# Stage A of a Fourier filter on quarters of the TensorE array: four matmuls per unit, eight units per batch

## The chip, the cores and the metric

The kernel runs on one core of one Trainium2 chip. A core has a matrix engine (TensorE, PE in the profile, with its weight loads as PEld), three engines for elementwise work (VectorE or DVE, ScalarE or ACT, GpSimd or POOL) and a queue processor, SyncE or SP, that issues DMAs here. The metric is the time of one execution on the device in microseconds; less is better. Every time below comes from runs of the kernel on the chip or from one profiled execution of it.

## The reference

A filter in the frequency domain along the sequence, and then a feed-forward network with a squared ReLU on all 24,064 tokens:

```python
batch, seq, dim = (8, 3008, 256)
X = np.fft.rfft(x, axis=1)
F = (filt_r + 1j * filt_i)[None, :, :]
y = np.fft.irfft(X * F, n=x.shape[1], axis=1).astype(np.float32)
...
h = np.maximum(y.reshape(24064, 256) @ w_in, 0.0)     # w_in 256 x 2048
out = (h * h @ w_out).astype(np.float32)              # w_out 2048 x 256
```

## The kernel before

The transform of length 3008 is split as 64 x 47. It runs per batch in stages, each of small matmuls by constant matrices, with a trip through memory where the data have to be laid out anew:

- **Stage A** is the transform of length 47. A row n of the sequence is cut as n = 64 n2 + 32 h + m, with n2 from 0 to 46, h of 0 or 1 and m from 0 to 31. A tile of x holds the 94 pairs (n2, h) in its partitions, and eight values of m with 256 channels each in its free dimension. The constant matrix `sSA` (94 x 96) has the same 47 x 48 block twice, one for each h, and zeros elsewhere. One unit is one matmul of 512 columns (two values of m) into one PSUM bank, and one copy to fp16. Four units fill a tile `u` of eight values of m (a chunk), which `write_u` stores to `dU` in memory. A batch has 16 units in four chunks.
- **Stage B** (`unit_b`, 12 units per batch) is the transform of length 64 on what `read_u` reads back: two matmuls of 256 columns into one bank, which VectorE multiplies with the filter; two accumulating DMAs from POOL's queue then add the halves.
- **Stage P** (`unit_p`, 12 units) is the first half of the inverse: two matmuls of 256 columns into one bank, a copy by ScalarE, a store to `dZ`.
- **Stage Y** (`unit_y`, 16 units) is the last transform: four matmuls of 94 columns into one bank, and a copy by ScalarE or VectorE into the operand `yt` of the network.

The network runs over 47 groups of 512 tokens, each in 8 slots. A slot s has the first product for one group (`ffn_g1`: four or more matmuls with 512 columns in all to each of two banks psH, then a ReLU by ScalarE, line 557), and a part of the second product for the group before it (`products`, 112 matmuls of 128 columns in the eight slots of a group; the sums that it needs, `sums`, and the squares, `ffn_sq`, are VectorE's).

The order of all engines' work is written out by hand, in the loop at the end: in each slot first `ffn_g1`, then a first place for units of the transform, then `products`, then a second place, then sums and squares. A place is half a slot. `fft_plan` fills the places: every unit has a due time in slots, at most one unit goes to a half-slot, the nearest free one, with a penalty for crowded neighbourhoods; units of stages B, P and Y are placed ahead of those of stage A. `moves` (loads of x, reads of `dU` and `dZ`) go to their half-slot without this limit. Batches 0 and 1 take stage A from wider tiles in the part before the loop; of batch 1 only four units of stage A are in the plan.

All units of the transform take their PSUM bank from one pool, `psF`, which has two banks and gives them in turn. The other six banks belong to `ffn_g1` (psH, twice two) and to the second product (psO, two). A unit's matmuls wait until the bank they are given has been read out by the unit that had it before.

x is loaded by POOL's DMA queue, which turns it to fp16 on the way: `load_x`, two DMAs for each chunk, each with 96 partitions and four values of m (a contiguous piece of 4 KB per partition); the last batch has 94 rows and cuts each in two. Stage A's copies are ScalarE's from batch 3 on, and by turns ScalarE's and VectorE's in batch 2. The stores of u go to the SP queue, one DMA of 96 partitions for each chunk.

Lines that matter below: 195 to 199 (loads of x), 208 (`sSA`), 340 to 343 (store of u), 358 (stage A's matmul), 362 and 364 (its copies), 442 and 450 (stage B's matmul and multiply), 487 and 489 (stage P), 523, 530 and 532 (stage Y), 553 and 557 (first product and ReLU), 564 (square), 639 to 648 (sums), 666 (second product), 710 to 719 (due times).

Of the kernel before, what the change touches and what calls it, by code (L numbers as in the profile page):

```python
# [9 lines left out]
F16 = mybir.dt.float16  # L10
# [8 lines left out]
N1, N2, NC, NM = 64, 47, 24, 32  # L19
# [7 lines left out]
def _build_consts():  # L27
    N = N1 * N2
    n2 = np.arange(N2)
    m = np.arange(NM)  # L30


    SA = np.zeros((N2, 2, 2, 2, NC))
    for c in range(NC):
        for h in range(2):
            SA[:, h, h, 0, c] = np.cos(2 * np.pi * n2 * c / N2)
            SA[:, h, h, 1, c] = np.sin(2 * np.pi * n2 * c / N2)

    S0 = np.zeros((128, 6, 2, 48))
    for h in range(2):
        q = SA[:, h, h].reshape(N2, 48)
        for t in range(2):
            S0[2 * h + t::4, t, h] = q[:32]
        for c in range(4):
            S0[4 * h + c:120:8, 2 + c, h] = q[32:]


    freq = np.full((NC, 64), -1)  # L50
    for c in range(NC):
        for j in range(32):
            freq[c, j] = 47 * j + c
            if c:
                freq[c, 32 + j] = 47 * j + 47 - c
    freq[0, 32] = N // 2


    SB = np.zeros((NM, 2, 2, NC, 2, 64))

    n1j = 8 * (m % 8) + 2 * (m // 8)
    SP = np.zeros((2, 64, NC, 2, 2, NM))
    for c in range(NC):
        for f in range(64):
            k = freq[c, f]
            if k < 0:
                continue
            sg = 1.0 if (f < 32 or c == 0) else -1.0
            for h in range(2):
                th = 2 * np.pi * ((k * (32 * h + m)) % N) / N  # L70
                SB[:, h, 0, c, 0, f] = np.cos(th)
                SB[:, h, 1, c, 0, f] = -sg * np.sin(th)
                SB[:, h, 0, c, 1, f] = -np.sin(th)
                SB[:, h, 1, c, 1, f] = -sg * np.cos(th)
            if c == 0 and f == 32:
                SB[:, :, 1, c, :, f] = 0.0
            w = (1.0 if k in (0, N // 2) else 2.0) / N
            for i in range(2):
                th = 2 * np.pi * ((k * (n1j + i)) % N) / N
                cs, sn = w * np.cos(th), w * np.sin(th)  # L80
                SP[0, f, c, i, 0] = cs
                SP[0, f, c, i, 1] = sg * sn
                SP[1, f, c, i, 0] = -sn
                SP[1, f, c, i, 1] = sg * cs


    SY = np.zeros((32, 2, 2, N2, 2))
    for c in range(NC):
        th = 2 * np.pi * c * n2 / N2
        for i in range(2):  # L90
            SY[c + c // 12 * 4, i, 0, :, i] = np.cos(th)
            SY[c + c // 12 * 4, i, 1, :, i] = -np.sin(th)


    PF = np.zeros((128, 6, 2, 2, 32))
    for w, (s, q) in enumerate(PQ):
        for j in range(32):
            PF[4 * j + q, w, :, s, j] = 1.0

    f16 = lambda a, p: np.ascontiguousarray(a.reshape(p, -1).astype(np.float16))  # L100
    C0 = np.zeros((128, 1472))
    C0[:, 0:576] = S0.reshape(128, 6, 2, 2, NC).transpose(0, 1, 4, 2, 3).reshape(128, 576)
    C0[:, 576:704] = np.eye(128)
    C0[:, 704:1280] = S0.reshape(128, 576)
    C0[0:94, 1280:1376] = SA.reshape(94, 96)
    C0[:, 1376:1470] = SY.reshape(128, 94)
    return f16(C0, 128), f16(PF, 128), f16(SB, 128), f16(SP, 128)

# [2 lines left out]
def kernel(  # L111
# [9 lines left out]
    nc = tc.nc  # L121
    B, S, D = x.shape
# [18 lines left out]
    p_x16 = ctx.enter_context(tc.tile_pool(name="p_x16", bufs=4))  # L141
    p_u = ctx.enter_context(tc.tile_pool(name="p_u", bufs=3))
# [10 lines left out]
    xrows = x.rearrange("b s d -> (b s) d")  # L153
    dU = [dram.tile([NM * 96, D], F16, name=f"dU{b}") for b in range(B)]
    dZ = [dram.tile([NM * 96, D], F16, name=f"dZ{b}") for b in range(B)]

    def psF(name):
        return pps.tile([128, 512], F32, tag="psF", name=name, bufs=2)
# [25 lines left out]
    x16s, us, uts, prods, zes, zts, yts = {}, {}, {}, {}, {}, {}, {}  # L184

    def load_x(b, k):

        c, i = divmod(k, 2)
        if i == 0:
            x16s[(b, c)] = p_x16.tile([96, 8, D], F16, tag="x16", name=f"x16_{b}_{c}")  # L190
        t = x16s[(b, c)][:, 4 * i:4 * i + 4, :]
        m = slice(8 * c + 4 * i, 8 * c + 4 * i + 4)
        if b + 1 < B:
            v = xrows[b * S:b * S + 96 * NM, :].rearrange("(p m) d -> p m d", m=NM)
            nc.gpsimd.dma_start(out=t, in_=v[:, m, :])
        else:
            v = xrows[b * S:b * S + S, :].rearrange("(p m) d -> p m d", m=NM)
            nc.gpsimd.dma_start(out=t[0:80], in_=v[0:80, m, :])
            nc.gpsimd.dma_start(out=t[80:94], in_=v[80:94, m, :])

    sC0 = p_t.tile([128, 1280], F16, tag="t", name="sC0")
    sC1 = const.tile([128, 192], F16, name="sC1")
    nc.scalar.dma_start(out=sC0[:, 0:704], in_=dC0.ap()[:, 0:704])
    s0 = sC0[:, 0:576].rearrange("p (w q) -> p w q", q=96)
    s1 = sC0[:, 704:1280].rearrange("p (w q) -> p w q", q=96)
    sSA = sC1[0:94, 0:96]
    sSY = sC1[0:112, 96:190]
    ident = sC0[:, 576:704]  # L210
    sPF = p_out.tile([128, 6, 128], F16, tag="ost", name="sPF")
# [1 line left out]
    xw32, xw16 = {}, {}  # L213
# [56 lines left out]
    ps = psO("warm").rearrange("p a d -> p (a d)")  # L270
# [67 lines left out]


    def write_u(b, c):  # L340
        nc.sync.dma_start(
            out=dU[b].rearrange("(m q) d -> q m d", q=96)[:, 8 * c:8 * c + 8, :],
            in_=us.pop((b, c)))

    def unit_a(b, a):

        c, i = divmod(a, 4)
        if i == 0:
            us[(b, c)] = p_u.tile([96, 8, D], F16, tag="u", name=f"u_{b}_{c}")
        ps = psF(f"psA_{b}_{a}")  # L350
        m = slice(2 * i, 2 * i + 2)
        if b == 1:
            nc.tensor.matmul(ps[0:96, :], s1[:, c // 2, :], xw16[(b, 2 * (c % 2))][:, m, :],
                             start=True, stop=False)
            nc.tensor.matmul(ps[0:96, :], s1[0:120, 2 + c, :], xw16[(b, 1)][0:120, m, :],
                             start=False, stop=True)
        else:
            nc.tensor.matmul(ps[0:96, :], sSA, x16s[(b, c)][0:94, m, :], start=True, stop=True)  # L358
        o = us[(b, c)][:, 2 * i:2 * i + 2, :]
        pv = ps[0:96, :].rearrange("p (a d) -> p a d", d=D)  # L360
        if a % 2 == 0 or b > 2:
            nc.scalar.copy(out=o, in_=pv)  # L362
        else:
            nc.vector.tensor_copy(out=o, in_=pv)
        if i == 3:
            write_u(b, c)

    def chunk_a(b, c):
# [323 lines left out]
    def fft_plan():  # L692

        fixed, units, moves = [], [], []
        for b in range(1, B):
            f = (b * S // TG) * SLOTS - (48 if b > 1 else 40)
            d = 0
            if b == 1:
                for n in range(4, 16):
                    fixed.append(((n if n < 8 else n + 2 if n < 12 else 2 * n - 7) + n % 2 / 2,  # L700
                                  unit_y, 0, n))
                moves.append((7.5, read_z, 0, 3))
                for k in range(4):
                    moves.append(((4.5, 5.5, 7.5, 7.5)[k], cast_wout, k, nc.vector))
                for a in range(12, 16):
                    fixed.append((2 + a / 2, unit_a, b, a))
                moves.append((10.5, read_u, b))
                d = 7
            else:
                for a in range(16):  # L710
                    if a % 2 == 0 and b > 2:
                        moves.append((f + ((-57 + 2.3 * a) if b == 3 else (-66 + 2.75 * a)),
                                      load_x, b, a // 2))
                    units.append((f + (-16 + a, -46 + 2.1 * a, -56 + 2.75 * a)[min(b, 4) - 2],
                                  unit_a, b, a))
                moves.append((f + (2 if b == 2 else -6.5), read_u, b))
            for p in range(12):
                r = 13.5 + 15 * p / 11 if b == 1 else 6 + 28 * p / 11 if b == 2 else -2 + 36 * p / 11
                units.append((f + r, unit_b, b, p))
                if b == 1 and 2 <= p < 10:  # L720
                    moves.append((f + r, load_x, 2, p - 2))
                units.append((f + r + (4.5 if b == 1 else 7 - 2.5 * p / 11), unit_p, b, p))
            for c in range(4):
                moves.append((f + (40 + d / 14, 43, 48, 54)[c] - d, read_z, b, c))
            for n in range(16):
                (fixed if n < 4 else units).append((f + YN[n] - d, unit_y, b, n))
        work, used, done = {}, set(), {}
        for r, *u in fixed:
            h = int(2 * r)
# [29 lines left out]
    for k in range(2):  # L759
        c = slice(12 * k, 12 * k + 12)  # L760
# [62 lines left out]
    for s in range((NG + 1) * SLOTS):  # L823
        g, k = divmod(s, SLOTS)
# [46 lines left out]
```

## Time and profile before

| what | value |
|---|---|
| median of 3 runs | 764.0 us (763.1 to 764.0) |
| the profiled execution, its own time | 765.4 us |
| its span, first to last instruction | 763.6 us |
| mean granted TensorE clock | 0.997 |
| stage A of batches 2 to 7 on TensorE (line 358) | 96 matmuls, 97 to 558 us into the span |
| its copies: ScalarE (line 362, with two of batch 1) / VectorE (line 364, with two of batch 1) | 90 of 580 ns / 10 of 681 ns |
| multiply of stage B (line 450) | 84 of 1219 ns |
| copy of stage P (line 489) | 84 of 584 ns |
| ReLU of the first product (line 557) | 376 of 1024 ns |
| load of x, issue to landing | median 5.0 us |
| DMA traffic | 109.26 MB, 143 GB/s in the mean |

A group of the profile is all instructions of one line, engine and shape: its count, its busy time, the mean time of one, and the time its engine was idle just before them with the instruction that ended the idle time. "PE psB L442" as a releaser means that the engine waited for the matmuls of line 442. The timeline lists instructions by their start, in microseconds from the start of the span. A matmul's duration is from its entry to its modelled end, and neighbours overlap: what it costs the stream is the distance to the next start.

### The profile page before, as it was taken

Reading aid. Unit: us, or ns where it says so; the run is one execution under the profiler, and the core shown is the slowest. Engines: PE = TensorE matmul, PEld = TensorE weight load, DVE = VectorE, ACT = ScalarE, POOL = GpSimd, SP = SyncE. Lnnn points to the kernel's source line nnn. Section 1 sums busy time; section 2 is a strip of 40 time slices with the busy share of each in tenths; the row PEclk is TensorE's granted clock in tenths of the full one; section 3 lists DMA queues with packets and bytes.
Section 4 is the critical chain, followed back from the end, with each engine's and each line's share of the span. In section 5 each row is a group of like instructions: output and inputs, shape, how many; then the busy total and the mean of one; then the engine's idle time right before and its main releaser. Section 6 shows DMA issues by size and latency. Waiting matters only on the chain.

```text
span 763.6 us, 19701 instructions
## 1 busy us (share of the span) xinstructions
PE 749.8 (98%) x8262; PEld 552.9 (72%) x8262; DVE 645.8 (85%) x714; ACT 578.8 (76%) x841; POOL 192.4 (25%) x260
## 2 busy tenths in 40 slices
PE   8988999999999999999999999999999999999998
PEld 5845766777777777877778777787777777777776
DVE  5857998899889888988979898798989989888783
ACT  3966777888877887788877877877877777777773
POOL 3800750244222321222312324033311222000000
PEclk9999999999999999999999999999999999999999
DMA  9985798765786467745585656775447334321011
GB/s 364 391 229 182 115 173 214 208 115 117 154 218 133 89 123 172 191 102 125 115 211 123 120 120 115 201 147 109 101 122 198 89 72 99 98 76 50 29 57 57
DMA packets 104946, 109.26 MB, mean 143 GB/s; under 512 B 9640, under 2 KB 93096, under 8 KB 102936
## 3 DMA queue, kind: packets, MB, share of 16 engines
q1 hardware_dynamic: 85704, 87.38, 37.1%
q0 software_dynamic: 19008, 20.43, 20.3%
q8 instruction: 65, 1.06, 0.6%
q14 instruction: 25, 0.20, 0.1%
q10 hardware_dynamic: 144, 0.18, 0.1%
HBM read 58.12 MB, written 48.23 MB: 139 GB/s over the span
## 4 chain that ended last, share of the span: by engine, by line
PE 88%; DVE 6%; DMA 3%; ACT 1%; issue 1%; POOL 0%; SPq 0%; ACTq 0%; DVEq 0%
PE psH L553 39%; PE psX L666 20%; PE psY L666 14%; PE psB L442 3%; PE psY L523 2%; PE psA L358 2%; PE psP L487 2%; DVE h L564 2%; PE psO L573 2%; DVE prod L450 1%; DMA ut<-dU 1%; PE warm L272 1%; DMA dU<-u 1%; PE psf L291 1%; PE psf L294 1%
## 5 line engine op out<-in xcount | busy, mean ns | idle before, releaser
L557 ACT ACTIVATE h<-psH 128x1024 f16<-128x1024 f32 x376 | 384.6, 1024 | 151.6 <-PE psH L553 147.4
L553 PE MATMUL psH<-yt,sWin 128*128 128x512 f16 (+7 forms) x1728 | 388.3, 352 | 1.4 <-DVE yt L532 0.6
L564 DVE TENSOR_TENSOR h<-h 128x2048 f16<-128x2048 f16 (+1 forms) x192 | 229.8, 1197 | 48.3 <-ACT h L557 48.0
L457 POOL DMA_DIRECT2D prod<-prod x168 | 138.6, 965 | 438.0 <-DVE prod L450 429.1
L553 PEld LDWEIGHTS <-sWin 128*128 128x128 f16 x1728 | 152.2, 98 | 99.4 <-issue 4.8
L666 PEld LDWEIGHTS <-sum 128*128 128x128 f16 x2880 | 177.5, 98 | 20.2 <-issue 0.2
L666 PEld LDWEIGHTS <-h 128*128 128x128 f16 x2160 | 133.6, 98 | 21.0
L450 DVE TENSOR_TENSOR prod<-psB,sF 128x1024 f16<-128x1024 f32 x84 | 102.4, 1219 | 16.4 <-PE psB L442 16.2
L666 PE MATMUL psX<-sT,sum 128*128 128x128 f16 x1440 | 102.5, 219 | 0.0
L666 PE MATMUL psY<-sT,sum 128*128 128x128 f16 x720 | 69.7, 219 | 0.0
L642 DVE TENSOR_TENSOR sum<-sum,h 128x2048 f16<-128x2048 f16 x45 | 55.0, 1222 | 1.0
L666 PE MATMUL psY<-sWout,h 128*128 128x128 f16 x720 | 55.0, 219 | 0.0
L666 PE MATMUL psX<-sT,h 128*128 128x128 f16 x720 | 54.9, 219 | 0.0
L666 PE MATMUL psY<-sWout,sum 128*128 128x128 f16 x720 | 54.7, 219 | 0.1
L645 DVE TENSOR_TENSOR sum<-h 128x2048 f16<-128x2048 f16 x45 | 54.8, 1217 | 0.0
L648 DVE TENSOR_TENSOR sum<-h,sum 128x2048 f16<-128x2048 f16 x45 | 54.7, 1217 | 0.0
L639 DVE TENSOR_TENSOR sum<-h 128x2048 f16<-128x2048 f16 x45 | 54.7, 1215 | 0.0
L362 ACT CAST u<-psA 96x512 f16<-96x512 f32 x90 | 52.2, 580 | 3.2 <-PE psA L358 2.8
L532 DVE CAST yt<-psY 128x376 f16<-128x376 f32 x62 | 33.7, 544 | 20.0 <-PE psY L523 19.9
L489 ACT CAST ze<-psP 128x512 f16<-128x512 f32 x84 | 48.9, 584 | 0.6 <-PE psP L487 0.4
L666 PE MATMUL psX<-sWout,h 128*128 128x128 f16 x720 | 47.6, 219 | 0.0
L523 PEld LDWEIGHTS <-zt 112*128 112x128 f16 x512 | 33.5, 98 | 18.5 <-issue 4.3
(86 smaller groups left out, 644.4 us busy)
## 6 DMA issues: line engine op xcount, KB each, us to landing
zt<-dZ SPq DMA_DIRECT2D x64, 192.0 KB
dU<-u SPq DMA_DIRECT2D x28, 384.0 KB
prod<-prod POOLq DMA_DIRECT2D x168, 64.0 KB, 2.7
dZ<-ze SPq DMA_DIRECT2D x28, 384.0 KB
x<-in_x_dram POOLq DMA_DIRECT2D x40, 192.0 KB, 5.0
ut<-dU SPq DMA_DIRECT2D x7, 1024.0 KB
xw<-in_x_dram SPq DMA_DIRECT2D x6, 1024.0 KB
out_dram<-top SPq DMA_DIRECT2D x31, 128.0 KB
```

The lines of the kernel that those rows point to most:

```text
L362: nc.scalar.copy(out=o, in_=pv)
L450: nc.vector.tensor_mul(out=prod, in0=ps.rearrange("p (a d) -> p a d", d=D).unsqueeze(1).to_broadcast([128, 2, 2, D]), in1=sF[:, :, 2 * p:2 ...
L457: nc.gpsimd.dma_start(out=prod[64 * i:64 * i + 64, 0], in_=prod[64 - 64 * i:128 - 64 * i, 1], accum_op=mybir.AluOpType.add)
L489: nc.scalar.copy(out=zes[(b, c)][:, 2 * i6:2 * i6 + 2, :], in_=ps.rearrange("p (a d) -> p a d", d=D))
L553: nc.tensor.matmul(ps[:, i, o:o + n], sWin[:, dt, jt * 128:(jt + 1) * 128], yts[b][:, dt, r:r + n], start=(dt == 0), stop=(dt == 1))
L557: nc.scalar.activation(out=h2[:, 2 * s:2 * s + 2, :], in_=ps, func=AF.Relu)
L564: nc.vector.tensor_mul(out=v, in0=v, in1=v)
L639: nc.vector.tensor_add(out=t, in0=a21, in1=a22)
L642: nc.vector.tensor_sub(out=t, in0=f[5], in1=a11)
L645: nc.vector.tensor_sub(out=t, in0=a11, in1=a21)
L648: nc.vector.tensor_sub(out=t, in0=a12, in1=f[6])
L666: nc.tensor.matmul(o[:, t, :], f[p][:, q, 128 * t:128 * t + 128], sg["w"][p][:, q, :], start=(m == 0 and p in (1, 2)), stop=(q == 7), skip ...
```

## The change

The array of TensorE is used in quarters in stage A of batches 2 to 7. The tile of x now has h = 0 in partitions 0 to 46 and h = 1 in partitions 64 to 110 (`load_x` issues one DMA for each h, of 48 partitions with eight values of m each; the last batch again in two pieces). The weight is the 47 x 48 block alone, once in each half of the partitions, with 16 columns of zeros to 64. A unit has four matmuls of 512 columns: for j of 0 and 1 (which four of the chunk's values of m) and h of 0 and 1. They read partitions from 64 h on and write PSUM partitions from 64 j on, h = 0 into a first bank of psF and h = 1 into a second one. Two copies follow, one for each bank, of 112 partitions by 512 elements. A chunk has two units, a batch eight in place of sixteen; in the plan they take the due times of the old units of odd number. `write_u` stores a chunk by two DMAs of 48 partitions. Batch 1 keeps the old unit under the name `unit_a1` and the old store, and its units of stages B and P, with the loads of x for batch 2 that go with them, come half a slot later (13.5 becomes 14).

```diff
@@ constants
-    C0[0:94, 1280:1376] = SA.reshape(94, 96)
+    for h in range(2):
+        C0[64 * h:64 * h + N2, 1280:1328] = SA[:, h, h].reshape(N2, 48)
...
-    sSA = sC1[0:94, 0:96]
+    sSA = sC1[:, 0:64]
@@ load_x
-        c, i = divmod(k, 2)
-        if i == 0:
-            x16s[(b, c)] = p_x16.tile([96, 8, D], F16, tag="x16", name=f"x16_{b}_{c}")
-        t = x16s[(b, c)][:, 4 * i:4 * i + 4, :]
-        m = slice(8 * c + 4 * i, 8 * c + 4 * i + 4)
-        if b + 1 < B:
-            v = xrows[b * S:b * S + 96 * NM, :].rearrange("(p m) d -> p m d", m=NM)
-            nc.gpsimd.dma_start(out=t, in_=v[:, m, :])
-        else:
-            v = xrows[b * S:b * S + S, :].rearrange("(p m) d -> p m d", m=NM)
-            nc.gpsimd.dma_start(out=t[0:80], in_=v[0:80, m, :])
-            nc.gpsimd.dma_start(out=t[80:94], in_=v[80:94, m, :])
+        c, h = divmod(k, 2)
+        if h == 0:
+            x16s[(b, c)] = p_x16.tile([112, 8, D], F16, tag="x16", name=f"x16_{b}_{c}")
+        t = x16s[(b, c)]
+        n = 48 if b + 1 < B else N2
+        v = xrows[b * S:b * S + 64 * n, :].rearrange("(n h m) d -> h n m d", h=2, m=NM)[h]
+        for p0, p1 in ((0, n),) if n == 48 else ((0, 32), (32, n)):
+            nc.gpsimd.dma_start(out=t[64 * h + p0:64 * h + p1],
+                                in_=v[p0:p1, 8 * c:8 * c + 8, :])
@@ write_u (b > 1)
+        v = dU[b].rearrange("(m q) d -> q m d", q=48)
+        for j in range(2):
+            m = 16 * c + 8 * j
+            nc.sync.dma_start(out=v[:, m:m + 8, :], in_=u[64 * j:64 * j + 48])
@@ unit_a
-            nc.tensor.matmul(ps[0:96, :], sSA, x16s[(b, c)][0:94, m, :], start=True, stop=True)
...
+    def unit_a(b, a):
+
+        c, i = divmod(a, 2)
+        if i == 0:
+            us[(b, c)] = p_u.tile([112, 8, D], F16, tag="u", name=f"u_{b}_{c}")
+        ps = [psF(f"psA_{b}_{a}_{h}") for h in range(2)]
+        for j in range(2):
+            m = slice(4 * j + 2 * i, 4 * j + 2 * i + 2)
+            for h in range(2):
+                p = slice(64 * h, 64 * h + N2)
+                nc.tensor.matmul(ps[h][64 * j:64 * j + 64, :], sSA[p], x16s[(b, c)][p, m, :],
+                                 start=True, stop=True)
+        for h in range(2):
+            o = us[(b, c)][:, 4 * i + h:4 * i + h + 3:2, :]
+            pv = ps[h][0:112, :].rearrange("p (a d) -> p a d", d=D)
+            if h == 0 or b > 2:
+                nc.scalar.copy(out=o, in_=pv)
+            else:
+                nc.vector.tensor_copy(out=o, in_=pv)
+        if i == 1:
+            write_u(b, c)
@@ fft_plan
-                    units.append((f + (-16 + a, -46 + 2.1 * a, -56 + 2.75 * a)[min(b, 4) - 2],
-                                  unit_a, b, a))
+                    if a % 2:
+                        units.append((f + (-16 + a, -46 + 2.1 * a, -56 + 2.75 * a)[min(b, 4) - 2],
+                                      unit_a, b, a // 2))
...
-                r = 13.5 + 15 * p / 11 if b == 1 else 6 + 28 * p / 11 if b == 2 else -2 + 36 * p / 11
+                r = 14 + 15 * p / 11 if b == 1 else 6 + 28 * p / 11 if b == 2 else -2 + 36 * p / 11
```

More of the change, by code (lines that the diff above doesn't have):

```diff
@@ L340, in write_u, with unit_a1 @@
     def write_u(b, c):
[L341 to L345, printed above, removed]
+        u = us.pop((b, c))
+        if b == 1:
+            nc.sync.dma_start(
+                out=dU[b].rearrange("(m q) d -> q m d", q=96)[:, 8 * c:8 * c + 8, :], in_=u)
+            return
+        v = dU[b].rearrange("(m q) d -> q m d", q=48)
+        for j in range(2):
+            m = 16 * c + 8 * j
+            nc.sync.dma_start(out=v[:, m:m + 8, :], in_=u[64 * j:64 * j + 48])
+    def unit_a1(b, a):
         c, i = divmod(a, 4)
@@ L351, in unit_a @@
         m = slice(2 * i, 2 * i + 2)
[L352 to L358, printed above, removed]
+        nc.tensor.matmul(ps[0:96, :], s1[:, c // 2, :], xw16[(b, 2 * (c % 2))][:, m, :],
+                         start=True, stop=False)
+        nc.tensor.matmul(ps[0:96, :], s1[0:120, 2 + c, :], xw16[(b, 1)][0:120, m, :],
+                         start=False, stop=True)
         o = us[(b, c)][:, 2 * i:2 * i + 2, :]
         pv = ps[0:96, :].rearrange("p (a d) -> p a d", d=D)
-        if a % 2 == 0 or b > 2:
+        if a % 2 == 0:
             nc.scalar.copy(out=o, in_=pv)
@@ L705, in fft_plan @@
                 for a in range(12, 16):
-                    fixed.append((2 + a / 2, unit_a, b, a))
+                    fixed.append((2 + a / 2, unit_a1, b, a))
                 moves.append((10.5, read_u, b))
```

## The prediction

> **What bounds the kernel now.** I read the page first: busy shares, then the chain that ended last.
>
> ```profile
> PE 749.8 (98%) x8262; PEld 552.9 (72%) x8262; DVE 645.8 (85%) x714; ACT 578.8 (76%) x841; POOL 192.4 (25%) x260
> ...
> PE 88%; DVE 6%; DMA 3%; ACT 1%; issue 1%; POOL 0%; SPq 0%; ACTq 0%; DVEq 0%
> ```
>
> TensorE is busy for 98% of the span and carries 88% of the chain. A busy share can hide slow matmuls, so I then asked for the chain in order of time, in the middle of the run:
>
> ```profile
> 381.63 0.86 PE psH L553 x4
> ...
> 384.25 0.89 PE psX L666 x16
> ```
>
> Four 512-column matmuls take 0.86 us (215 ns each), sixteen of 128 columns 0.89 us (56 ns each). I take these as the rate of a dense stream. The table of windows shows that the stream has no holes where the changed units run (97 to 558 us):
>
> ```profile
> 200.00:290.00 90.00, 89.85 (x1015) 66.53 (x1013) 78.59 (x86) 71.89 (x108) 23.41 (x32) 1.00 0.64 144
> 290.00:381.00 91.00, 90.85 (x1030) 68.17 (x1028) 79.87 (x88) 72.85 (x109) 24.05 (x32) 1.00 0.62 140
> ```
>
> The columns are stage, length, busy time of PE, PEld, DVE, ACT and POOL, clock and DMA. In 181 us TensorE lacks 0.3 us; DVE has 12% left, ACT 20%. So here a nanosecond taken from the matmul stream is a nanosecond of the total, and a nanosecond that TensorE waits is lost and nothing makes it good. The changed group is small in it (the groups by line: busy us, mean ns, idle time before and its releaser; with it the copy that empties its bank, and stage B's multiply):
>
> ```profile
> L450 DVE TENSOR_TENSOR prod<-psB,sF 128x1024 f16<-128x1024 f32 x84 | 102.4, 1219 | 16.4 <-PE psB L442 16.2
> ...
> L362 ACT CAST u<-psA 96x512 f16<-96x512 f32 x90 | 52.2, 580 | 3.2 <-PE psA L358 2.8
> ...
> L358 PE MATMUL psA<-x,sC 94*96 94x512 f16 x96 | 36.6, 381 | 0.2 <-DVE u L364 0.2
> ```
>
> The 381 ns is one matmul from entry to modelled end; the stream advances 215 ns. The 96 matmuls hold TensorE for 96 x 215 = 20.6 us, and each waits for almost nothing (0.2 us in all). Last, the timeline, because the new unit takes both psF banks at once and there are only two. This is a stage-B unit followed one half-slot later by a stage-A unit of an odd number, which is where the change puts a new unit:
>
> ```profile
> 243.70 1.22 DVE L645 TENSOR_TENSOR sum<-h 128x2048 f16<-128x2048 f16 x1
> 243.71 0.38 PE L442 MATMUL psB<-ut,sSB 128*128 128x256 f16 x2
> ...
> 244.71 0.38 PE L358 MATMUL psA<-x,sC 94*96 94x512 f16 x1
> ...
> 244.84 1.22 DVE L450 TENSOR_TENSOR prod<-psB,sF 128x1024 f16<-128x1024 f32 x1
> 244.93 1.03 PE L553 MATMUL psH<-yt,sWin 128*128 128x512 f16 x4
> ...
> 246.11 0.33 PE L523 MATMUL psY<-sC,zt 112*128 112x94 f16 x4 [0.15 <-DVE prod L450]
> ```
>
> The A matmul starts at 244.71, when the bank of the B unit is still full: VectorE reads it until 244.84 + 1.22 = 246.06. It doesn't matter today, since A has the other bank. The next unit (Y) needs B's bank, and it starts at 246.11, 0.05 us after VectorE is done and 0.15 us late. That is the price of a bank in this kernel, seen once.
>
> **What the Trainium skill says.** "TensorE: Matmul & The Clock Gate", Part 3: matmuls in different row and column tiles run at the same time, span about one matmul plus 4 ns for each further tile (a packing of 16 at 512 columns measured 10.6 times faster). "TensorEngine Tiling (Array Packing)", Key Properties: a change of tiling mode drains TensorE; Restrictions: column tiling loses the fast weight load; Performance Considerations, PSUM Bottleneck: tiling speeds up the matmuls and not the reading of PSUM. No matmul of the trace before is tiled (the smallest has 94 rows and 96 columns), so it shows neither overlap nor drain. On weights it agrees as far as it goes: 96 columns take 123 ns to load, 128 columns 98.
>
> **The change, part by part.** The sum is made against the profiled execution, 765.4 us (span 763.6); the median of the runs is 764.0, so 1.4 us is taken off at the end.
>
> *Matmuls.* Removed: 96 x 215 ns = 20.6 us. Added: 48 quads of 512 columns. Bounds of one quad: 215 + 3 x 4 = 227 ns if all four overlap, 4 x 215 = 860 ns if none do. I take 227, since the four use four different quarters and the first page measures this; 48 x 227 = 10.9 us. Gain 9.7 us.
>
> *Entering and leaving the quarter mode.* Each quad stands between full-array matmuls, so there are 96 switches. Lower bound 0. Upper bound of one: the tail of a matmul past its stream time, 381 - 215 = 166 ns, so 16 us for 96. I take half, 83 ns each[...]; 8.0 us. Where the quad waits for a bank anyway the entry is covered; that is about half of the units (below), 24 x 83 ns = 2.0 us. Cost 6.0 us. The weights (four loads of 64 columns in place of two of 96) are taken to come ahead in this; if they don't, it lies inside the upper bound.
>
> *The wait for the second bank.* This is the term that decides. A unit now needs the bank of the unit directly before it, whose eviction was until now free to end a unit later. The planner keeps the odd places of A (unit k at the old place 2k+1), so I took the old odd-numbered A matmuls and asked, in the timeline, when the eviction of the psF unit before them ends. In batches 4 to 7 the pattern is the same each time. Batch 4: after B at 220.39, eviction ends 0.76 us after A's start; after P at 231.99, 0.48; after B at 243.71, 246.06 - 244.71 = 1.35; after B at 274.70 (A at 275.70, VectorE from 276.17 to 277.39), 1.69; the other four have their bank. Sum 4.28 us, times four batches 17.1. Batch 3 by the same reading 3.7, batch 2 1.3 (its units are moved by the planner, so this is rough). Together 22.1 us in some 20 units, 18.2 of it behind B.
> Ends: if VectorE were free at every B, the wait would be 0.20 us from matmul to VectorE, plus 1.22, less 0.89 of matmuls until A, 0.53 us; with 15 such pairs 8 us. At the other end 22.1 plus 0.05 us of latency for each, 23. I take 20: VectorE's queue comes mostly from the FFN's sums and squares, which move along with TensorE, and only a little of it is worked off while TensorE waits. Behind the waiting quad stands the whole matmul stream, so nothing covers it.
>
> *The bank after the quad.* The next unit needs the first of the two banks, freed by the first copy. It comes 0.9 to 1.1 us later, while matmul to end of copy is 0.78 us with ScalarE free and 1.47 behind a psH activation. Today the odd A units show such late ends by 0.1 to 0.7 us in about a third of the cases. After a bank wait ScalarE is idle, so I take 1.5 us in all; bounds 0 and 4.
>
> *What costs nothing.* The copies: 16 per batch as before, 112 in place of 96 partitions, 512 elements each, so 580 ns again, two in a row; the psH banks absorb 0.58 us more, for ScalarE has 20% left. The stores of u: two DMAs of 48 partitions in place of one, 24 more issues of some 0.32 us on the SP queue, which waits for most of its time (25.9 us for these copies alone), and the read of u is far behind. The loads of x: the same number and bytes, 48 partitions with 8 KB rows; the first unit of a chunk now needs both halves, which are issued about seven slots earlier (a slot is 0.86 + 0.89 = 1.75 us of the chain above, so 12 us), and a landing takes 5.0 us. Batch 1's B and P units half a slot later: nothing waits for them within a slot. The constants: same DMA.
>
> Sum: 765.4 - 9.7 + 6.0 + 20 + 1.5 = 783.2 us by the profiled run; less 1.4, 782.
>
> **Rivals.**
> *R1, the bank wait decides (the forecast):* 782, with its own range 772 to 793 from the ends above (waits 12 to 23, switches 2 to 12). For it: the 1.35 and 1.69 us read off above, and no slack on TensorE. Against it: VectorE might run ahead once TensorE waits.
> *R2, the quad itself is dear as well:* the four quarters run in pairs (430 ns), or the narrow weight loads stand in front of each. For pairs the gain of 9.7 is gone, 792; with none overlapping a quad of 860 ns replaces two matmuls of 430, 48 x 430 ns = 20.6 us worse than before, so 764 + 20.6 + 20 + 1.5 = 806 with free switches. For it: the two column groups share rows; against it: the page's measurement.
> *R3, faster:* the quad runs as one, and the bank wait stays small, because a waiting TensorE lets VectorE and ScalarE empty their queues, and the next B is read at once. Place: the B-A pairs; price: what is left of the waits. The point: waits, switches and follow-ups together under 9.7 us, 0.2 us per unit. With 6 us left, 760. Against it: the floor of 8 us for B-A pairs with a free VectorE.
> *R4, between:* free switches and waits near the floor, 764 - 9.7 + 10 to 14, 765 to 770.
>
> **How the numbers follow.** R1 0.58, R2 0.20, R3 0.07, R4 0.15. A measurement of this kernel can tell about 0.2% (1.5 us) from no change. Faster is R3: 0.07; same is the lower edge of R4: 0.04; slower is the rest, 0.89. R1's range reaches up into the pairs of R2 and down into R4 until a tenth is left on each side: 767 to 800.
>
> **What would show it.** TensorE idle before the quad, released by the multiply of L450, in pieces of 0.5 to 1.7 us and some 15 to 20 us in all, and by the copies of P for 2 to 3 us; its busy share falls to about 95 to 96%. The starts of the quad's four matmuls tell overlap (a few ns apart, the next matmul some 220 ns later) from pairs or single file; the time from the matmul before to the quad, where no bank is missing, is the switch. The forecast is wrong if the four matmuls stand 215 ns apart, if idle time before them adds up to less than 10 us, or if another wait (x, SP, psH) appears.

## The result and the profile after

The changed kernel takes 787.4 us (median of 4 runs, 786.9 to 788.3), against 764.0 before: a ratio of 1.0307, 95% interval 1.0289 to 1.0325. It is slower by 23.4 us. Its profiled execution took 787.0 us, its span 785.2. Lines after the change are some twenty numbers higher: the quad is line 377, its copies 383 and 385, stage B's multiply 471, the first product 574, the square 585, the sums 660 to 669, the second product 687.

The busy shares and the chain, from the page of the changed kernel:

```profile
PE 756.8 (96%) x8358; PEld 548.7 (70%) x8358; DVE 647.7 (82%) x714; ACT 578.0 (74%) x841; POOL 191.8 (24%) x260
...
PE 80%; DVE 12%; DMA 3%; ACT 2%; issue 2%; POOL 0%; ACTq 0%; SPq 0%; DVEq 0%; POOLq 0%
```

TensorE's busy share falls from 98% to 96%, and VectorE's part of the chain doubles from 6% to 12%. No other engine has much more to do than before: VectorE has 647.7 us in place of 645.8, ScalarE 578.0 in place of 578.8. What grew is waiting. The table of windows, for the same two stages as before:

```profile
200.00:290.00 90.00, 86.81 (x985) 62.99 (x983) 74.99 (x81) 68.25 (x104) 22.33 (x30) 1.00 0.60 135
290.00:381.00 91.00, 88.06 (x995) 64.35 (x993) 77.57 (x85) 68.81 (x103) 22.91 (x32) 1.00 0.59 136
```

TensorE now lacks 6.1 us in 181 us, where it lacked 0.3. Who ended those waits stands in the group of the new matmuls:

```profile
L377 PE MATMUL psA<-x,sC 47*64 47x512 f16 x192 | 28.7, 397 | 14.6 <-DVE prod L471 13.7 <-DVE yt L553 0.4 <-DMA prod<-prod 0.2
```

Of 14.6 us idle just before a matmul of line 377, 13.7 us ended with stage B's multiply. The idle time understates the loss. The first matmul of a quad gets in, and counts as busy for its 0.40 us, while the other three wait. In the timeline of one such unit (TensorE alone, then VectorE alone) both can be seen:

```profile
249.36 0.38 PE L463 MATMUL psB<-ut,sSB 128*128 128x256 f16 x2
...
249.92 0.61 PE L687 MATMUL psX<-sT,sum 128*128 128x128 f16 x8
250.46 0.40 PE L377 MATMUL psA<-x,sC 47*64 47x512 f16 x1
251.98 0.41 PE L377 MATMUL psA<-x,sC 47*64 47x512 f16 x3 [1.13 <-DVE prod L471]
252.32 0.39 PE L574 MATMUL psH<-yt,sWin 128*128 128x512 f16 x1
```

```profile
249.58 1.22 DVE L666 TENSOR_TENSOR sum<-h 128x2048 f16<-128x2048 f16 x1
250.72 1.22 DVE L471 TENSOR_TENSOR prod<-psB,sF 128x1024 f16<-128x1024 f32 x1
```

It is the unit of the prediction's timeline (B at 243.71 before). The first matmul of the quad starts at 250.46 in the bank that is free; the other three start at 251.98, when VectorE has read B's bank (250.72 + 1.22 = 251.94). Between them lie 1.52 us, of which the profile calls 1.13 idle. Summed over the 48 quads, the distance from the first start to the second is 23.7 us. Without a wait it is 4 ns, so the second bank cost 23.5 us in 23 units.

A quad that has both banks looks like this:

```profile
260.56 0.83 PE L687 MATMUL psY<-sWout,sum 128*128 128x128 f16 x12
261.32 0.41 PE L377 MATMUL psA<-x,sC 47*64 47x512 f16 x4
261.66 0.60 PE L574 MATMUL psH<-yt,sWin 128*128 128x512 f16 x2
```

The twelve matmuls before it stream until 260.56 + 12 x 0.056 = 261.23. The quad starts 93 ns later. Its four starts lie within 10 ns, and the next full-array matmul starts 333 ns after the last of them, where 216 ns would be the stream. So a quad takes 93 + 10 + 333 = 436 ns of TensorE. The two matmuls that it replaces took 2 x 215 = 430 ns at the rate of a dense stream, and 2 x 220 = 440 if they are measured as the quad is, to the start of the next matmul (219 to 221 ns each). The overlap of the quarters is complete, and entering and leaving the mode eats all of it.

In sum the quads take 44.4 us from the end of the stream before them to the start of the one after. The old matmuls took 21.5 by the same measure, with one wait of 0.4 us in it. That is 22.9 us of the loss.

The spans differ by less, 21.6 us, because the changed kernel's execution is ahead when the quads begin: the same matmul of the first product starts at 93.94 us before and at 90.29 after. Two causes can be seen. The profiled execution of the kernel before (765.4 us, above its median) has a mean granted clock of 0.66 between 49 and 54 us, the other one has 1.00 there. And before, a stage-B unit of batch 1, at 74.14 us, waits for its read of dU (1.3 us in the view of waits, 1.5 by the starts). In the changed kernel, where these units come half a slot later, TensorE doesn't wait for dU at all. From there to the end it loses 25.3 us. Outside the quads a stage-Y unit waits 1.6 us, by the starts, for a read of dZ, and three P units wait 1.0 us together for a quad's copies.

### The profile page after: what moved, and what is told of

Same layout as the page of the kernel before. It is cut to its first block, busy times and chain, and to the rows that moved or that the text cites. A ratio compares the mean times of both kernels' runs of the same rounds, so it can differ in the third digit from the quotient of the medians.

```text
span 785.2 us, 19908 instructions
## 1 busy us (share of the span) xinstructions
PE 756.8 (96%) x8358; PEld 548.7 (70%) x8358; DVE 647.7 (82%) x714; ACT 578.0 (74%) x841; POOL 191.8 (24%) x260
## 4 chain that ended last, share of the span: by engine, by line
PE 80%; DVE 12%; DMA 3%; ACT 2%; issue 2%; POOL 0%; ACTq 0%; SPq 0%; DVEq 0%; POOLq 0%
PE psH L574 36%; PE psX L687 18%; PE psY L687 13%; DVE prod L471 4%; DVE h L585 3%; PE psA L377 2%; PE psY L544 2%; PE psB L463 2%; PE psP L508 2%; PE psO L594 2%; DVE sum L666 1%; ACT h L578 1%; DMA prod<-prod 1%; DVE sum L660 1%; PE warm L268 1%
## 5 line engine op out<-in xcount | busy, mean ns | idle before, releaser
L574 PEld LDWEIGHTS <-sWin 128*128 128x128 f16 x1728 | 148.4, 98 | 98.2 <-issue 10.3
L383 ACT CAST u<-psA 112x512 f16<-112x512 f32 x88 | 47.5, 588 | 23.7 <-PE psA L377 23.1
L196 POOL DMA_DIRECT2D x<-in_x_dram x56 | 51.9, 1114 | 0.2 <-issue 0.2
```

Of the source, the lines that this page charges most:

```text
L196: nc.gpsimd.dma_start(out=t[64 * h + p0:64 * h + p1], in_=v[p0:p1, 8 * c:8 * c + 8, :])
L574: nc.tensor.matmul(ps[:, i, o:o + n], sWin[:, dt, jt * 128:(jt + 1) * 128], yts[b][:, dt, r:r + n], start=(dt == 0), stop=(dt == 1))
```

## The experiments

The medians, each with the kernel before on the same chip:

| version | us | before | ratio (95%) |
|---|---|---|---|
| two full-array matmuls per unit, two psF banks | 781.1 | 763.6 | 1.0229 (1.0199 to 1.0259) |
| quarter mode, one bank per unit | 783.4 | 763.6 | 1.0255 (1.0240 to 1.0270) |
| quads at quiet places | 773.9 | 763.6 | 1.0137 (1.0118 to 1.0157) |
| quads on psH | 765.5 | 763.6 | 1.0021 (1.0010 to 1.0032) |
| the same, first place of a slot only | 766.4 | 764.1 | 1.0033 (1.0022 to 1.0045) |
| batch 1 half a slot later, alone | 764.1 | 764.1 | 0.9997 (0.9988 to 1.0006) |
| row tiles without column tiles | 772.9 | 764.1 | 1.0111 (1.0098 to 1.0124) |
| two quads per visit, psH and psF | 782.7 | 764.1 | 1.0243 (1.0226 to 1.0259) |
| the same at quiet places | 771.4 | 763.9 | 1.0100 (1.0084 to 1.0115) |
| and the copies split | 767.0 | 763.9 | 1.0037 (1.0024 to 1.0051) |
| and one more place avoided | 761.4 | 764.8 | 0.9965 (0.9954 to 0.9977) |
| that version with full-array matmuls | 763.0 | 764.2 | 0.9988 (0.9979 to 0.9998) |

Theory W says that the wait for the second psF bank is the loss. Its rival, theory Q, says that it is the quarter mode itself (a dear quad, or a stream that it disturbs), and that the banks only show it.

### The banks without the quarter mode

```diff
+        ps = [psF(f"psA_{b}_{a}_{h}") for h in range(2)]
+        for h in range(2):
+            m = slice(4 * i + 2 * h, 4 * i + 2 * h + 2)
+            nc.tensor.matmul(ps[h][0:96, :], sSA, x16s[(b, c)][0:94, m, :], start=True, stop=True)
```

> Two matmuls of the full array per unit (94 rows, 96 columns, as before), one in each of the two psF banks, eight units per batch at the changed kernel's places; x, weights and stores as before. No quarter mode at all. Theory W (the wait for the second bank is the whole loss): 23 to 24 us of TensorE idle before the second matmul again, 785 to 789 us. Theory Q (the quarter mode is the loss, and the banks only show it): near 764 us, 768 at most.

It took 781.1 us. Theory Q (768 at most) is out: most of the loss is there with not one tiled matmul. But theory W's number was 4 to 8 us too high. The timeline of TensorE at the same unit shows one reason:

```profile
250.43 0.38 PE L373 MATMUL psA<-x,sC 94*96 94x512 f16 x1
252.05 0.38 PE L373 MATMUL psA<-x,sC 94*96 94x512 f16 x1 [1.24 <-DVE prod L466]
252.27 0.60 PE L569 MATMUL psH<-yt,sWin 128*128 128x512 f16 x2
```

The bank comes at nearly the same time (252.05), but here half of the unit's work was done during the wait, and 0.22 us after it the stream goes on. In the quad three quarters of the work remain, and they take as long as all four, 0.34 us with the exit. So a wait in the middle of a packed group also costs the overlap of the group: 0.12 us in each of 23 units, 2.7 us in all.

Summed over the units the lost time is 16.5 us here and 23.5 there. The other 4.4 us of the difference lie in five units, and have another reason (the view of waits, and the timeline of VectorE and TensorE at one of them):

```profile
PE psA L373 <- ACT u L378: 3.3, 5, 0.7
...
283.19 1.22 DVE L466 TENSOR_TENSOR prod<-psB,sF 128x1024 f16<-128x1024 f32 x1
283.55 0.38 PE L373 MATMUL psA<-x,sC 94*96 94x512 f16 x1 [0.67 <-ACT u L378]
```

The second matmul starts at 283.55, right after ScalarE's copy of the unit's own first matmul, while VectorE still reads the bank of the unit before it until 284.41. It took the first matmul's bank again. So psF doesn't always give its banks in turn, and in five of the 48 units this run doesn't hold two banks. In the quad, whose third matmul still writes to the first bank, these units wait 0.8 to 0.9 us longer.

### The quarter mode without the second bank

```diff
-        ps = [psF(f"psA_{b}_{a}_{h}") for h in range(2)]
-        for j in range(2):
...
+        ps = psF(f"psA_{b}_{a}")
+        p = slice(64 * h, 64 * h + N2)
+        for j in range(2):
+            m = slice(4 * j + 2 * i, 4 * j + 2 * i + 2)
+            nc.tensor.matmul(ps[64 * j:64 * j + 64, :], sSA[p], x16s[(b, c)][p, m, :],
+                             start=True, stop=True)
```

with h from the unit's number, 16 units per batch at the old places (and 13.5 for batch 1).

> Quarter mode with one bank: a unit is two matmuls, the two column groups of one h, 16 units per batch at the places of the kernel before. Theory W: no wait for a bank, but 96 visits to the quarter mode at 93 ns in, 4 ns between the two and 333 ns to the next stream, 430 ns in place of 216, so 96 x 0.214 = 20.5 us more, 783 to 786 us, with idle time released by VectorE under 2 us. If two column groups on the same rows don't overlap: 640 ns each, 803 to 807. If the wait for the bank came from the quarter mode, idle before line 377 of 10 us or more is seen here too.

It took 783.4 us, as theory W has it, and no bank is missing:

```profile
L377 PE MATMUL psA<-x,sC 47*64 47x512 f16 x192 | 38.7, 400 | 0.0
```

The idle time before the tiled matmuls is 0.0 us. 95 of the 96 pairs took 93 + 4 + 333 ns to within 2 ns (one came 65 ns later), 41.3 us in place of 21.5. The price of a visit is thus 93 ns in and 117 ns out, the same for two tiles as for four, whatever stands before and after it. The starts of the two column groups are 4 ns apart although they read the same rows.

### Quads at places where the bank is free

```diff
+                    + (u[0] is unit_a and u[1] > 2) * (20 * (h - 1 in used) + 20 * (h - 2 in isb)
+                                                       + 4 * (h + 1 in used)))
```

in the planner's choice of a half-slot (`isb` holds those of stage B).

> The changed kernel, but from batch 3 on the planner puts a quad where no psF unit stands one half-slot before it, and no stage-B unit two before it. Theory W: the waits go from 23.5 to some 3 to 5 us (batch 2 and one unit of batch 3 keep theirs), and a quad with its switches costs what two matmuls cost, 436 ns for 432: 766 to 770 us. Theory Q: 780 us or more.

It took 773.9 us, 13.5 less than the changed kernel, but 4 us more than expected. The waits inside the quads fell from 23.5 to 6.1 us. Not counted was the wait of others for the quad's own two banks, in the view of waits:

```profile
PE psA L377 <- DVE prod L471: 3.1, 3, 1.5
PE psB L463 <- ACT u L383: 2.8, 6, 0.5
```

A stage-B unit after a quad now waits up to 0.5 us for its second copy; by the starts these six waits are 3.8 us, and with the 6.1 they nearly make up the 10.3 us that are left. With two banks and a unit that holds both, the turn is tight on both sides.

### Quads on other banks

```diff
-        ps = [psF(f"psA_{b}_{a}_{h}") for h in range(2)]
+        t = psH(f"psA_{b}_{a}")
+        ps = [t[:, 0, :], t[:, 1, :]]
...
+        o = us[(b, c)][:, 4 * i:4 * i + 4, :].rearrange("p (a h) d -> p h a d", h=2)
+        pv = t[0:112].rearrange("p h (a d) -> p h a d", d=D)
+        if b > 2 or i == 0:
+            nc.scalar.copy(out=o, in_=pv)
+        else:
+            nc.vector.tensor_copy(out=o, in_=pv)
```

with the copy of every second unit of batch 2 on VectorE.

> The changed kernel with the quad's two banks taken from psH, as one tile of two banks, and one copy of 112 x 1024 in place of two of 112 x 512. The psF turn is left alone. Theory W: no wait for a psF bank, 436 ns for 432 per quad, ScalarE 48 x 0.15 us less busy: 763 to 767 us; waits for a psH bank of 0 to 3 us would come on top. Theory Q: 780 us or more.

It took 765.5 us. The matmuls, the mode, the layout of x and the stores are those of the changed kernel; only the banks and the shape of the copy differ. 22 us are gone. This is the plainest sign that the turn of psF was the cost, and that the tiled matmuls alone are worth nothing either way. Its quads take 22.1 us in all, 1.2 us over 48 x 0.436, and the excess is in 11 units of the second place of a slot, after which the stream starts 57 to 169 ns late.

The same with the first place only (`+ (u[0] is unit_a) * 20 * (h % 2)` in the planner's choice):

> The kernel with quads on psH, but only in the first place of a slot (after the first product, before the second), so that the second product's 0.9 us stand between the quad and the next psH tile. The trace of the quads on psH shows exits of 390 to 502 ns in place of 333 in about a dozen units, all in the second place. Theory: they go, 1.2 us less: 763.5 to 765 us, as before the change. Rival: they have another cause and stay: 765.5.

The late exits went, each of the 48 quads takes 434 to 437 ns, and yet the median is 766.4 us, above the expected 765. The view of waits of its profile has one new wait:

```profile
PE psY L544 <- DMA zt<-dZ: 3.4, 2, 2.1
```

A stage-Y unit waited up to 2.1 us for a read of dZ (1.7 us in all with the quads on psH). What made it late was not followed up. Right after it the mean granted clock is 0.63 from 125 to 127 us and 0.76 from 127 to 131. And the late exits that went were no gain: by the starts, 25 first products (line 574) now begin 45 to 275 ns late behind a ReLU, 2.4 us in all, where with the quads on psH seven such delays made 0.9 us beside the 1.2 us of late exits. The view of waits shows next to nothing of this, since TensorE still counts as busy with the matmul before. So the wait for a psH bank moved rather than went.

### The part of the change in batch 1

```diff
-                r = 13.5 + 15 * p / 11 if b == 1 else ...
+                r = 14 + 15 * p / 11 if b == 1 else ...
```

> The kernel before with one part of the change alone: batch 1's units of stages B and P, and the loads of x for batch 2 beside them, half a slot later. Theory: this part does nothing by itself, 763 to 765 us. Rival: the 2 us that the changed kernel's quads cost over its whole loss come from it, 761 to 762 us.

764.1 us for both, so this part does nothing by itself that 14 runs can tell. Its profile shows two sides. The wait for dU at 74 us is gone, as it is in the changed kernel; the one-bank run, which has 13.5, still has it (1.2 us). But here a P unit waits 0.9 us for the multiply, at 100.63, and a later stage-B unit 1.1 us for its dU, at 140.52. So the half slot is a part of the changed kernel's early lead, and alone it leaves nothing.

### Row tiles alone

```diff
-    sSA = sC1[:, 0:64]
+    sSA = (sC1[:, 64:176], sC1[:, 0:112])
...
-                nc.tensor.matmul(ps[h][64 * j:64 * j + 64, :], sSA[p], x16s[(b, c)][p, m, :],
-                                 start=True, stop=True)
+                nc.tensor.matmul(ps[h][0:112, :], sSA[j][p], x16s[(b, c)][p, m, :],
+                                 start=(j == 0), stop=(j == 1))
```

> Row tiles without column tiles: the four matmuls of a quad have weights of 112 columns (the block at columns 0 or 64 and zeros elsewhere), so the two of one h add up in one bank and only the two h overlap; banks from psH in the first place as in the run beside it. If entering and leaving costs 93 + 117 ns for row tiles as well: 93 + 216 + 4 + 333 = 646 ns in place of 430, 10 us more, 773 to 776 us. If only column tiles pay it: 435 ns, 763.5 to 766 us. If rows don't overlap either: 860 ns, 784 us or more.

It took 772.9 us, just under the range of the first case. Each unit takes 93 ns to enter, and 665 ns in all. Row tiles pay for the switch too: 93 ns in and 92 ns out here, and the second pair starts 260 ns after the first rather than 216.

### Two quads in one visit

```diff
+        t = psH(f"psA_{b}_{c}")
+        pss = ([t[:, 0, :], t[:, 1, :]], [psF(f"psA_{b}_{c}_{h}") for h in range(2)])
+        for i, ps in enumerate(pss):
+            for j in range(2):
+                m = slice(4 * j + 2 * i, 4 * j + 2 * i + 2)
...
+        nc.scalar.copy(out=u[:, 0:4, :].rearrange("p (a h) d -> p h a d", h=2),
+                       in_=t[0:112].rearrange("p h (a d) -> p h a d", d=D))
...
```

> Two quads in one visit to the quarter mode: a unit is a whole chunk, four per batch, the first quad into a psH tile with one copy, the second into the two psF banks, at the first place of a slot and away from psF units where the planner can. If a visit costs 93 ns in and 117 ns out however many quads it holds: 93 + 216 + 10 + 333 = 652 ns in place of four matmuls at 215, 0.21 us less in each of 24 visits, 5 us; some 2 to 4 us of waits for psF in batches 2 and 3 remain: 760 to 764 us. If the price is paid per quad: 764 to 768. If the burst of three copies holds up the ReLU and so psH: above 768.

The quads are those of the changed kernel; the two psF copies follow that of the psH tile. It took 782.7 us, a miss by 19. The 18 undisturbed visits did as expected, 651 to 653 ns; six wait 0.4 to 1.2 us for their own second psF bank. But the copies come in a burst of 1.01 + 1.09 us behind a ReLU of 1.02, and the next psF unit meets them. The timeline of TensorE and ScalarE:

```profile
332.67 0.63 PE L378 MATMUL psA<-x,sC 47*64 47x512 f16 x8
332.78 1.02 ACT L580 ACTIVATE h<-psH 128x1024 f16<-128x1024 f32 x1 [0.32 <-PE psH L576]
...
333.70 1.01 ACT L380 CAST u<-psA 112x1024 f16<-112x1024 f32 x1
334.59 1.09 ACT L386 CAST u<-psA 112x512 f16<-112x512 f32 x2
335.24 0.38 PE L465 MATMUL psB<-ut,sSB 128*128 128x256 f16 x2 [1.17 <-ACT u L386]
```

The matmuls were done at 333.3; B gets its bank at 335.24, 2 us later, and waits 1.17 us for it. In the whole run B waits 10.8 us for line 386. The third case named a time above 768, but not this cause: what waits is the next psF unit, not the ReLU's psH.

Two steps follow from this. First other places (`+ 10 * (h + 1 in used)` in place of 4, in batch 2 no preference but the first place of a slot, and a wider search):

> Two quads in one visit, as in the run of two quads, but from batch 3 on at places with no psF unit one half-slot before or after where one exists. In that run the visits themselves saved what was expected and stage B then waited for the copies (10.8 us behind line 386). Theory (the two psF copies end too late for the next psF units, being last of a burst of three): fewer units stand close behind, a part of that goes, 768 to 778 us. Rival (the burst holds up the ReLU wherever it stands): 780 us or more.

771.4 us; B's wait for line 386 fell to 1.5 us. The rival is out. Then another order of the copies, with VectorE taking one bank:

```diff
+        nc.scalar.copy(out=ous[0], in_=pvs[0])
+        nc.vector.tensor_copy(out=ous[1], in_=pvs[1])
+        nc.scalar.copy(out=u[:, 0:4, :].rearrange("p (a h) d -> p h a d", h=2),
+                       in_=t[0:112].rearrange("p h (a d) -> p h a d", d=D))
```

> The same places, with the copies in another order: first the psF bank of h = 0 on ScalarE, that of h = 1 on VectorE beside it, and the psH tile last on ScalarE. Theory: the psF banks come free 1.0 us and 1.6 us sooner, the waits of stage B behind these copies fall to 2 us or less and the 5 us of the shared visits come out: 760 to 767 us, at the low end faster than the kernel before. Rival (the burst and VectorE's queue just move the wait): 770 us or more.

767.0 us, at the upper end of the range and still slower than before. B's wait behind these copies has fallen to 0.3 us in the view. What is left there is the quad's own wait, behind a stage-Y unit that VectorE empties:

```profile
PE psA L378 <- DVE yt L552: 3.3, 4, 0.8
```

By the starts, one visit in each of batches 4 to 7 waits 1.19 us. The last step avoids that place (`if u[0] is unit_b or u[0] is unit_y and u[2] % 2`):

> The kernel with two quads in one visit and the copies split, with one place more avoided: no stage-Y unit that VectorE empties two half-slots before a visit. In the run before it one visit of each of batches 4 to 7, and one of batch 3 with half as much, waits 1.2 us for VectorE's copy of such a unit; the planner now moves those of batches 4 to 7 by three slots. Theory (every us of bank wait taken away comes out of the total): 4 x 1.2 = 4.8 us less, 761 to 764 us, equal to or faster than the kernel before. Rival (the wait just moves to the next unit that VectorE empties): 765 us or more.

761.4 us, ratio 0.9965 (0.9954 to 0.9977): 0.35% faster than the kernel before, and 26 us faster than the change as it was made. The visits take 18.0 us in all, 4.8 less than in the run before it. A visit at the new place in the timeline of TensorE:

```profile
263.50 0.63 PE L378 MATMUL psA<-x,sC 47*64 47x512 f16 x8
264.06 0.40 PE L686 MATMUL psY<-sWout,h 128*128 128x128 f16 x4
```

Eight matmuls stand in 0.56 us. By its page ScalarE is busy for 566.6 us, 12 less than before, and VectorE for 654.3, 8.5 more. The control has the same places, banks and copies with the old matmuls:

> The control to the fastest version: the same units, places, banks and order of copies, but the four matmuls of a unit are those of the kernel before (full array, 94 rows, 96 columns), with its x, weights and stores; no quarter mode. Theory (the 5 us come from sharing one visit between two quads, 652 ns in place of 4 x 215 = 860): 24 x 0.21 = 5.0 us slower than that version, 765 to 767 us; as the second pair comes to its banks 0.1 us later, waits shrink by up to 1 us, so 764 at the low end. Rival (the gain comes from the new places and banks): 761 to 763 us.

763.0 us, ratio 0.9988 (0.9979 to 0.9998). That is the upper end of the rival's range, but neither side has it whole. The quarter mode brings 1.6 us between the medians, which come from two chips, and 1.8 by the ratios; the places, banks and copies, with batch 1's half slot, which both versions have, bring about 1 us. The visits in the control take 21.2 us, 3.2 more than with quads, where 5.0 were expected: the quads come to their psF banks sooner and still wait 0.28 us in each of batches 4 to 7, 0.39 in batch 2 and 0.65 in batch 3, the full-array matmuls only 0.4 us in all. Of the 3.2 us the medians show half. Two parts of the rest can be seen in the views of waits: stage-Y units waiting for dZ (2.5 us with quads, 1.1 in the control) and the second product waiting for ScalarE's copy of its sums (line 695, 0.7 us in four places, none in the control).

## Why the prediction was right

**The sign and the deciding term.** The forecast was that the wait for the second bank decides, 782 us, range 767 to 800. It is 787.4. The step "the wait for the second bank" was read at 22.1 us, and 20 were taken. Read in the same way, from the end of the stream before the unit to the second start, it measured 25.7: the 23.5 between the first start and the second, and 93 ns of entry in each of the 23 units, which pass while the bank is awaited anyway. Taking less than was read was the error, and the reading itself was too low, for VectorE came later than before, not earlier: in the unit shown its multiply starts 0.35 us after the stream's end (249.92 + 8 x 0.056 = 250.37), where before it was 0.13 us (244.71 to 244.84). The four waits of batches 4 to 7, read as 0.76, 0.48, 1.35 and 1.69, came as 0.81, 0.53, 1.62 and 1.96. Removing that wait by other banks took away 22 us (quads on psH), and the wait without the quarter mode made 17.5 us by itself (two full-array matmuls).

**The matmuls.** "227 ns if all four overlap" held: starts within 10 ns, 216 ns of stream. This agrees with the 4 ns per tile of "TensorE: Matmul & The Clock Gate", Part 3. The gain of 9.7 us is there; by the starts it is 48 x (440 - 226) ns = 10.3 us.

**The switches.** This term was mis-sized: 6.0 us were taken, at 83 ns each with half of the entries covered. They are 93 ns in and 117 ns out. Half of the entries are covered, as was taken, so the term is 25 x 93 + 48 x 117 ns = 7.9 us. Quads that wait for no bank come out even with the old matmuls (436 ns for 440), where the prediction had a gain of 3.7 us in all. The price is within the bounds that the prediction drew (0 to 166 ns). That it is the drain which "TensorEngine Tiling (Array Packing)", Key Properties, names is not shown. The weights were taken to come ahead, and they don't: the four loads of the quad at 261.32 start with its matmuls, where in the stream a load starts some 60 ns earlier (275.64 for the matmul at 275.70, before). No run separates the two.

**The bank after the quad.** 1.5 us were taken. The view of waits of the changed kernel has 0.5 us behind line 383, and the starts have 1.0 us in three P units, so it was smaller here. It became large only where a quad was followed closely and its copies came in a burst.

**What was costed at nothing** mostly stayed there: copies 588 ns in place of 580, and the stores on SP and the loads of x appear in no wait of TensorE. Batch 1's half slot was no zero in this kernel: "nothing waits for them within a slot" missed that TensorE waited 1.5 us, by the starts, for dU at their old place.

**The sum.** The terms made 17.8 us. Measured they make 24.3 (-10.3 + 7.9 + 25.7 + 1.0): 5.7 us too little for the waits and 1.9 for the switches, 0.5 too much for what follows, and 0.6 too little for the gain. What the sum left out goes both ways. The wait for dU is gone (1.5 us), and so is the old wait of a Y unit, which by the starts is 0.32 us at 246.11 and comes once in each of batches 4 to 7 (1.3 us); a Y unit's wait for dZ came in (1.6 us). That makes 23.1, and 23.4 is the difference of the medians. The low end of the first rival's own range was added up wrongly: with waits of 12 us and switches of 2 its terms give 770, not 772.

**The signs.** Idle time before the quad released by the multiply is 13.7 us, under the 15 to 20 us named, and none is seen that P's copies released, where 2 to 3 us were named. Five units do wait behind P, 0.44 us each by the starts, but the first matmul of the quad counts as busy for most of that.

The rivals: the dear quad (pairs, or single file) is out by the starts. The faster case had the point "0.2 us per unit for waits, switches and follow-ups together". Switches alone are 0.21, so a quad by itself could hardly have won; two in one visit could, and did.

## What to carry to other kernels

Before packing matmuls, count banks: a unit that takes every bank of its pool is released by the unit directly before it. In the dense TensorE stream of this kernel that wait was lost in full, with the overlap of the packed group on top. Read its size beforehand from the timeline, as the end of the previous unit's eviction less the start of the unit, and don't discount it. Look at starts, too, and not at idle time alone, which showed 14.6 of the 23.5 us here. A visit to a tiled mode costs about 0.2 us here, as much as one 512-column matmul, so one quad of quarters gains nothing and two in a row gain one matmul's time, as long as the copies behind them don't hold the banks that others need.

## What the runs showed of the hardware that was not expected

- The price of entering and leaving a tiled mode is constant to a few ns: 93 ns in, 117 ns out for 64 x 64 quarters with two or four tiles in use, after 128- or 512-column matmuls alike; 93 and 92 ns for row tiles with 112 columns, whose second pair starts 260 ns after the first.
- A second quad in the same mode stands 240 ns after the first rather than 216, and the exit is then 92 ns (117 where the second quad waited for its bank); a visit of two quads takes 652 ns, as the sum of single prices had it.
- Narrower weights don't load faster: the 64 columns of a quarter take 103 ns, the 112 of a row tile 125, 96 columns of the full array 123, and its 128 columns 98. All four loads of a quad stand within 0.11 us.
